# A gated MLP block with local attention on one core: 7-for-8 in the first projection, reloads and stores on another DMA queue, and the last two matrix products exchanged

## The chip, the cores and the metric

The kernel runs on 1 core of a Trainium2 chip. The metric is device time in microseconds (us), lower is better. Each kernel is run several times, beside the kernel before on the same chip.

Engine names follow the profile. PE is TensorE (matmul), PEld its weight loads, DVE VectorE, ACT ScalarE, POOL GpSimd, SP SyncE. A `q` after a name (SPq, ACTq) is that engine's instruction queue issuing a DMA.

## The reference, cut to what matters

```python
# x: [1, 2048, 1024]   wqkv: [1024, 3072]   wo: [1024, 1024]   w1, w3: [1024, 3584]   w2: [3584, 1024]   all bf16
def reference(x, wqkv, wo, w1, w3, w2):
    xn = _layernorm(x)
    q, k, v = split_heads(xn @ wqkv)                 # 32 heads of 32
    # each position sees 8 keys: itself, 2 back, 4 back, ... 14 back
    attn = softmax(mask(einsum("bhsd,bhswd->bhsw", q, k[idx]) * Dh ** -0.5))
    s = einsum("bhsw,bhswd->bhsd", attn, v[idx]) @ wo
    h = silu(xn @ w1) * (xn @ w3)
    g = silu(h @ w2)
    return x + s * g
```

## The kernel before

All large products use a 7-for-8 scheme: a 2x2 block product needs seven block products, if the sums of blocks (`s1`..`s4`, `t1`..`t4`) have been formed on VectorE. The exception is q of the first two chunks of 512 tokens (`q_plain`). The work runs in this order. "Half" is 1024 tokens.

```python
    for st in range(NST):                                  # head: normalise and transpose chunk 0
        ln_tp(0, st, [(xT[:, 0:2], slice(0, 2))], ...)
    q_plain(0, wq0, wq1, ...); q_plain(1, wq0, wq1, ...)   # first q: eight products of eight
    qkv_seven(1, 0, ...) ... qkv_seven(0, 1, ...)          # k, v and the second q
    mlp_up(0, {1: att_step, 6: att_step})                  # "up", half 0; attention runs beside it on DVE
    mlp_down(0)
    att_step()
    wo(0)
    mlp_up(1, {0: att_step, 7: att_step})
    mlp_down(1)
    wo(1)                                                  # the last product
```

First, q, k and v of later chunks are parked in DRAM and reloaded, 1 MB each, on the SP queue. That queue also carries all weight loads. In the trace SP waits 6.6 us there for the copy on POOL that the vT load needs, and issues the loads of q and of weights only after it, at 277.85 and 278.62 us. The code of the reloads:

```python
    def fetch_k(c):
        ...
        nc.gpsimd.tensor_copy(out=kT[:, :, 0:HALO], in_=kT[:, :, CH:CH + HALO])
        nc.sync.dma_start(out=kT[:, :, HALO:], in_=k_dram[c])
        qt[c] = att_tile((NJ, CH), BF16, f"qt{c}")
        nc.sync.dma_start(out=qt[c][:], in_=q_dram[c])

    def fetch_v(c):
        nc.gpsimd.tensor_copy(out=vT[:, :, 0:HALO], in_=vT[:, :, CH:CH + HALO])
        nc.sync.dma_start(out=vT[:, :, HALO:], in_=v_dram[c])
```

Second, in up of half 0 the weights are loaded, summed on VectorE, used, and the sums stored for half 1:

```python
        nc.sync.dma_start(out=wt[:, 0], in_=w1_r[:, :, fc])       # 512 KB; w3 alike
        ...
            nc.vector.tensor_add(st[:, 0], wt[:, 1, 0:KH], wt[:, 1, KH:KT])   # ... four sums
        nc.gpsimd.dma_start(out=s_dram[fb], in_=st[:])            # 1 MB
```

Third, the end of each output tile of `wo`. The store is issued by ScalarE, and the residual x is loaded into a tile that it shares with the product:

```python
        def finish(u, dh, gp, ps, add=None):
            ...
            xo = (k4 if b == 0 else a4)(f"xo{b}{u}{dh}{gp}", (2, 2, CH), BF16)
            nc.sync.dma_start(out=xo[:, 0], in_=rows_(x_flat))
            with hp():
                ...                                               # xo[:, 1] = the product
                nc.vector.tensor_mul(g, xo[:, 1], g)
                nc.vector.tensor_add(g, g, xo[:, 0])
                nc.scalar.dma_start(out=rows_(out_flat), in_=g)
```

## Time and profile before

The median is 767.7 us (3 runs, 765.62 to 767.78). The profiled execution spans 765.8 us. The first lines of its page: busy time of PE, then the span in 40 slices of 19.1 us, in tenths (PE busy, granted PE clock, DMA engines busy).

```profile
...
PE 727.2 (95%) x3381; PEld 352.9 (46%) x3436; DVE 603.0 (79%) x573; ACT 328.5 (43%) x346; POOL 72.7 (9%) x104
...
PE   7999999989999998999999999799999999999994
...
PEclk8999999999999999999999999899999999999998
DMA  9342454574686799969748868445367546453413
...
```

PE is busy 95% of the span. Its row dips in one inner slice, the 26th (479 to 498 us), where the clock row dips too, and in the last. So the time can fall only where PE stands still, runs at half clock, or does work that can be left out. I cut the span into stages at the first matmul of each. Here are three stages of before. The columns are: window, its length, then busy time and instruction count of PE, PEld, DVE, ACT and POOL, then the granted clock, DMA share and GB/s.

```profile
...
core 0: us, PE busy (x) PEld busy (x) DVE busy (x) ACT busy (x) POOL busy (x), PEclk, DMA share, GB/s
173.82:356.06 182.24, 171.98 (x780) 76.25 (x793) 175.06 (x180) 89.70 (x88) 26.34 (x37) 1.00 0.77 257
467.97:645.27 177.30, 170.20 (x770) 76.50 (x784) 152.51 (x117) 90.42 (x89) 9.46 (x17) 0.98 0.55 172
755.78:765.81 10.03, 0.17 (x1) 0.00 (x0) 4.76 (x8) 1.93 (x2) 0.00 (x0) 0.76 0.63 210
...
```

Up of half 0 lasts 182.24 us, with VectorE busy 175.06. Up of half 1 does the same products in 177.30 us. The tail, in which PE has nothing left to do, is 10.03 us. In this trace matmuls with 512 columns start 0.2157 us apart at a granted clock of 1.00, which is called full clock here, and 0.427 us apart at 0.50, half clock (13.3 to 16.9 us). A *stop* in this document is what the spacing of two weight loads exceeds 0.2157 us by.

Where PE waits in the stretch of up of half 0 around 268 to 307 us, and where VectorE does. The columns of the waits view: who waited for whom, us in total, times, longest.

```profile
...
PE em L136 <- DVE st L493: 3.0, 1, 3.0
PE am L136 <- DMA w<-in_B_w_dram: 0.9, 1, 0.9
```

```profile
...
DVE st L493 <- DMA w<-in_B_w_dram: 3.6, 1, 3.6
...
```

The 3.0 us wait for weight sums (`st`) is VectorE's 3.6 us wait for a weight load, passed on. The queues show what that load stood behind. This is the timeline of SP's queue and of POOL in this stretch: start, length, instruction.

```profile
...
277.28 0.53 SPq L365 DMA_DIRECT2D vT<-v_dram  x1
277.85 0.66 SPq L361 DMA_DIRECT2D qt<-q_dram  x1
278.62 0.37 SPq L480 DMA_DIRECT2D w<-in_B_w_dram  x1
...
```

```profile
...
270.75 6.50 POOL L364 COPY vT<-vT 128x128 bf16<-128x128 bf16 x1 [1.51 <-DVE C L412]
...
```

The reload of vT waits for a 6.50 us copy on POOL. The weight load at 278.62 comes behind it and behind the reload of q.

At the border from wo to up of half 1, first ACT, then PE:

```profile
...
479.67 1.48 ACTq L716 DMA_DIRECT2D out_dram<-h_sb  x3
485.50 1.00 ACT L146 COPY bm<-am 128x1024 f32<-128x1024 f32 x1 [8.44 <-DMA out_dram<-h_sb]
...
```

```profile
...
470.44 8.40 DMA xo<-in_A_x_dram
...
479.63 1.15 DVE pt L374
...
484.19 1.23 DVE um L525
...
485.50 1.00 ACT bm L146
...
```

```profile
...
486.55 2.29 PE L136 MATMUL am<-xT,w 128*128 128x512 bf16 x5 [4.55 <-ACT bm L146]
489.06 1.06 PE L136 MATMUL am<-xT,w 128*128 128x512 bf16 x2 [0.22 <-issue]
...
```

ACT stands idle for 8.44 us before the copy that PE needs. In its queue ahead of the copy are three output stores, which wait for VectorE. They are issued from 479.67 to 481.14 us. The bracket names the one of several semaphores that the profile puts last; the chain shows what released the copy at 485.50: VectorE's addition `um`, which ends at 485.42. VectorE itself had waited 3.1 us for a load of residual x (issued at 470.44, 8.40 us to land), and then ran the scores of attention chunk 3 (`pt`, `Es`) ahead of `um`. PE waits 4.55 us and then runs at half clock (granted clock 0.50 from about 484.6 to 491.4 us): its next eight matmuls (eight weight loads; one matmul record is missing) fill 486.55 to 489.92 us, where 8 x 0.2157 us is 1.7. The end of the kernel:

```profile
...
752.33 3.62 PE L136 MATMUL wb<-wt,oT 128*128 128x512 f16 x16
...
756.17 0.97 SPq L708 DMA_DIRECT2D xo<-in_A_x_dram  x2
...
760.28 0.69 DVE L715 TENSOR_TENSOR h_sb<-h_sb,xo 128x1024 bf16<-128x1024 bf16 x1 [0.38 <-DMA xo<-in_A_x_dram]
```

The last two loads of residual x are issued only at 756.17, after PE has finished, because their tiles were in use until then (SP waits 13.7 us there for VectorE's addition, L715). The last addition waits 0.38 us for one.

### The profile page before, as it was taken

The numbers are of one execution on the slowest core, as the hardware profiler recorded it, in microseconds if no ns is written. First come the engines' busy times: TensorE is split into PE (matmuls) and PEld (weight loads), VectorE is DVE, ScalarE is ACT, GpSimd is POOL, SyncE is SP. The second block draws the span as 40 slices with busy tenths as digits, with TensorE's granted clock in tenths as the row PEclk, the third lists the DMA queues.
The fourth block names the chain that finished last, engine by engine and source line by source line (L and its number), as shares of the span: only waits on it lengthen the run. The fifth ranks groups of instructions, "written<-read, shape, count | busy, mean of one in ns | idle before, by whom it ended". The sixth has DMA issues, their size and how long they took to land.

```text
span 765.8 us, 8592 instructions
## 1 busy us (share of the span) xinstructions
PE 727.2 (95%) x3381; PEld 352.9 (46%) x3436; DVE 603.0 (79%) x573; ACT 328.5 (43%) x346; POOL 72.7 (9%) x104
## 2 busy tenths in 40 slices
PE   7999999989999998999999999799999999999994
PEld 3666655554444343444444444344444444444442
DVE  7825997699999998999999568899993699711426
ACT  4786433534444455544121254354565453121232
POOL 0000000130000042300061004000004000000000
PEclk8999999999999999999999999899999999999998
DMA  9342454574686799969748868445367546453413
GB/s 338 115 171 119 179 178 151 158 226 141 228 274 224 217 315 316 286 240 334 258 151 278 312 194 244 138 152 149 140 193 209 175 150 207 145 188 118 140 55 111
DMA packets 115928, 151.56 MB, mean 198 GB/s; under 512 B 4912, under 2 KB 94512, under 8 KB 110000
## 3 DMA queue, kind: packets, MB, share of 16 engines
q1 hardware_dynamic: 101280, 111.16, 45.0%
q0 software_dynamic: 5072, 26.22, 9.7%
q10 hardware_dynamic: 9536, 13.63, 5.0%
q8 instruction: 27, 0.44, 0.3%
q14 instruction: 13, 0.11, 0.0%
HBM read 107.48 MB, written 39.32 MB: 192 GB/s over the span
## 4 chain that ended last, share of the span: by engine, by line
PE 51%; DVE 26%; issue 10%; DMA 9%; ACT 2%; POOL 1%; SPq 0%; ACTq 0%; DVEq 0%; POOLq 0%
PE db L136 9%; PE bm L136 7%; PE de L136 6%; PE da L136 5%; DVE pt L373 4%; PE am L136 4%; PE em L136 4%; DMA w<-in_B_w_dram 4%; PE qp L136 4%; PE bq L136 3%; DVE pt L374 3%; PE aq L136 2%; PE eq L136 2%; DVE um L525 2%; DVE h_sb L535 2%
## 5 line engine op out<-in xcount | busy, mean ns | idle before, releaser
L136 PEld LDWEIGHTS <-h_sb 128*128 128x128 f16 (+1 forms) x944 | 98.9, 105 | 108.6 <-issue 4.9
L136 PEld LDWEIGHTS <-st 128*128 128x128 f16 x896 | 86.9, 98 | 112.0 <-DVE st L493 8.4
L136 PE MATMUL am<-xT,w 128*128 128x512 bf16 x425 | 106.3, 383 | 8.4 <-ACT bm L146 5.3
L136 PEld LDWEIGHTS <-w 128*128 128x128 bf16 x672 | 66.0, 99 | 94.0 <-issue 15.4
L136 PE MATMUL bm<-xs,st 128*128 128x512 f16 x448 | 105.8, 379 | 0.2
L373 DVE TENSOR_TENSOR pt<-qt,kT 128x4096 bf16<-128x4096 bf16 x32 | 73.2, 2287 | 0.5
L136 PE MATMUL db<-wt,h_sb 128*128 128x512 f16 x336 | 73.2, 379 | 0.0
L136 PEld LDWEIGHTS <-wq 128*128 128x128 bf16 (+1 forms) x352 | 50.4, 144 | 31.7 <-issue 7.3
L527 ACT ACTIVATE g<-um 128x1024 bf16<-128x1024 f32 x28 | 29.6, 1057 | 74.3 <-DVE um L525 74.2
L136 PE MATMUL bm<-xs,w 128*128 128x512 f16 x224 | 55.4, 383 | 3.5 <-DVE h_sb L535 3.4
L136 PE MATMUL em<-xs,st 128*128 128x512 f16 x224 | 53.2, 379 | 3.9 <-DVE st L493 3.9
L136 PE MATMUL em<-xT,st 128*128 128x512 bf16 x218 | 52.4, 379 | 0.3
L543 DVE TENSOR_TENSOR h_sb<-h_sb,g 128x2048 bf16<-128x2048 bf16 x28 | 34.1, 1218 | 20.2 <-ACT g L542 20.2
L136 PE MATMUL da<-wt,h_sb 128*128 128x512 bf16 x219 | 48.9, 379 | 0.6 <-DMA wt<-in_B_w_dram 0.3
L405 POOL DMA_DIRECT2D Ep<-pb x64 | 36.9, 584 | 84.8 <-DVE pb L401 81.5
L146 ACT COPY pm<-em 128x1024 f32<-128x1024 f32 x28 | 28.4, 1013 | 28.8 <-PE em L136 28.8
L374 DVE TENSOR_TENSOR pt<-pt 128x2048 bf16<-128x2048 bf16 x32 | 39.0, 1218 | 0.3
L521 ACT ACTIVATE h_sb<-am 128x1024 bf16<-128x1024 f32 x28 | 28.6, 1023 | 20.0 <-PE am L136 20.0
L525 DVE TENSOR_TENSOR um<-em,um 128x1024 f32<-128x1024 f32 x28 | 34.1, 1216 | 3.8 <-PE em L136 2.5
L146 ACT COPY bm<-am 128x1024 f32<-128x1024 f32 x28 | 28.0, 1000 | 20.9 <-DMA out_dram<-h_sb 8.4
L146 ACT COPY um<-bm 128x1024 f32<-128x1024 f32 x28 | 28.4, 1013 | 19.2 <-PE bm L136 19.2
L412 DVE TENSOR_TENSOR B<-Ep,vT 128x4096 bf16<-128x4096 bf16 x16 | 36.5, 2282 | 0.0
(161 smaller groups left out, 978.4 us busy)
## 6 DMA issues: line engine op xcount, KB each, us to landing
w<-in_B_w_dram SPq DMA_DIRECT2D x42, 512.0 KB, 5.3
s_dram<-st POOLq DMA_DIRECT2D x14, 1024.0 KB, 5.1
wt<-t_dram SPq DMA_DIRECT2D x16, 896.0 KB, 6.5
st<-s_dram SPq DMA_DIRECT2D x14, 1024.0 KB, 5.0
wt<-in_B_w_dram SPq DMA_DIRECT2D x12, 896.0 KB, 6.4
w2q<-in_B_w_dram SPq DMA_DIRECT2D x14, 512.0 KB, 4.6
t_dram<-w2q POOLq DMA_DIRECT2D x7, 1024.0 KB, 5.2
wq<-in_A_wqkv_dram SPq DMA_DIRECT2D x6, 1024.0 KB, 7.7
```

What stands on the lines that cost most here:

```text
L136: nc.tensor.matmul(ps, lhsT=lhs[k], rhs=rhs[k], start=(first and k == 0), stop=(k == n - 1), skip_group_check=not first,)
L146: nc.scalar.copy(out=out_, in_=in_)
L373: nc.vector.tensor_mul(p_t[:], q[:], kT[:, :, o:o + CH])
L374: nc.vector.tensor_add(p_t[:, 0:4, :], p_t[:, 0:4, :], p_t[:, 4:8, :])
L405: nc.gpsimd.dma_start(out=pr[c][r:P:NR, :, sq * P:(sq + 1) * P], in_=pb[sq * 32:(sq + 1) * 32, :, :])
L412: nc.vector.tensor_mul(dst, E[:, w, :].unsqueeze(1).to_broadcast([P, NJ, CH]), vT[:, :, o:o + CH])
L521: nc.scalar.activation(out=h_sb[:, f2, 0:CH], in_=pa[:], func=ACTF.Silu)
L525: m = nc.vector.tensor_add(su2[:], pe[:], su2[:])
L527: nc.scalar.activation(out=hl["g"][:, :, CH:], in_=su2[:], func=ACTF.Silu)
L535: m = nc.vector.tensor_add(h_sb[:, f2, CH:], pb[:], sp5[:])
L543: nc.vector.tensor_mul(h_sb[:, f2, :], h_sb[:, f2, :], hl["g"][:])
```

## The change

Its intent: use the 7-for-8 scheme for the first q as well, which takes 16 matmuls out; put the last `wo` ahead of the last down, so that the kernel ends on a cheaper finish; get the reloads out of the weight loads' queue and the early stores out of ScalarE's queue (both go to POOL's queue, which the profile lists as software_dynamic: 26.22 MB in before); and keep PE's clock up with dummy matmuls before the first q. The diff, cut to its core (the renamings and the splitting of `wo` into `wo_prepare` and `wo` are left out):

```diff
+    def spin(ps, n):                        # dummies
+        for k in range(n):
+            nc.tensor.matmul(ps[:, k % 2], lhsT=warm[:, 0:P], rhs=warm[:], start=True, stop=True)
...
     def ln_tp(c, st, dst, busy=0):
         tp = bank2(f"tp{c}_{st}")
+        spin(tp, busy)                      # 5, 0, 1, 1 for the four tiles of chunk 0
...
-        nc.sync.dma_start(out=kT[:, :, HALO:], in_=k_dram[c])
+        nc.gpsimd.dma_start(out=kT[:, :, HALO:], in_=k_dram[c])
...
-        nc.sync.dma_start(out=qt[c][:], in_=q_dram[c])
+        nc.gpsimd.dma_start(out=qt[c][:], in_=q_dram[c])
...
-        nc.sync.dma_start(out=vT[:, :, HALO:], in_=v_dram[c])
+        nc.gpsimd.dma_start(out=vT[:, :, HALO:], in_=v_dram[c])
...  # att_steps: the attention of chunks 2 and 3
         with priority(BG + 20000):
             softmax(2)
+        yield
+        with priority(BG + 30000), behind("wo"):     # not before wo's VectorE work
             scores(3)
-        yield
-        with priority(BG + 30000):
-            values(2)
-            fetch_v(3)
+            values(2, (0, 2, 4))
...  # finish of wo, half 0: x is loaded ahead into its own tile
+        d = h_sb[:, 16 + 2 * n:18 + 2 * n, CH:]
         with hp():
+            to_bf16(d, ps, add)
+            anchor["wo"] = nc.vector.tensor_mul(g, d, g)
+            nc.vector.tensor_add(g, g, xw[u, dh][:, gp])
-            nc.scalar.dma_start(out=rows_(out_flat), in_=g)
+            nc.gpsimd.dma_start(out=out_rows(out_flat, 0, u, dh, gp), in_=g)
...  # finish of the last down; the wo product waits in so, the residual in xr
+    def gated(u, dh, gp, i_=slice(0, 2)):
+        g = g_tile(1, u, dh, gp)[:, i_]
+        with hp():
+            nc.vector.tensor_mul(g, so[u][:, dh, gp, i_], g)
+            nc.vector.tensor_add(g, g, xr[u][:, dh, gp, i_])
+            nc.sync.dma_start(out=out_rows(out_flat, 1, u, dh, gp)[:, i_], in_=g)
...  # head
-    q_plain(0, wq0, wq1, xk(xT[:, 0], xT[:, 1]), mid1)
-    q_plain(1, wq0, wq1, xk(b12[:], xT[:, 2]))
+    for t, (w0, w1_, ws) in enumerate(((wq0, wq1, sq), (wk0, wk1, sk))):
+        first_two(...)                      # a11*b11 + a12*b21 for q and k: needs chunk 0 alone
+    qkv_seven(0, 0, wq0, wq1, sq, None, snap[0:2])
...
-    nc.sync.dma_start(out=x_dram[:, 0:2], in_=xT1[:, 0:2])      # three stores, to gpsimd
+    nc.gpsimd.dma_start(out=x_dram[:, 0:2], in_=xT1[:, 0:2])
...
-    mlp_up(1, {0: att_step, 7: att_step})
-    mlp_down(1)
-    wo(1)
+    mlp_up(1, {0: att_step, 6: att_step})
+    wo_prepare(1)
+    wo(1, finish1)
+    residual()
+    mlp_down(1, gated)
```

More of the change, by code (lines that the diff above doesn't have):

```diff
@@ L126 @@
     nc.vector.memset(warm[:], 0.0)
+    def spin(ps, n):
+        for k in range(n):
+            nc.tensor.matmul(ps[:, k % 2], lhsT=warm[:, 0:P], rhs=warm[:], start=True, stop=True)
     for i in range(4):
-        wps = bank2(f"warm{i}")
-        for h in range(2):
-            for _ in range(2 if i < 2 else 1):
-                nc.tensor.matmul(wps[:, h], lhsT=warm[:, 0:P], rhs=warm[:], start=True, stop=True)
+        spin(bank2(f"warm{i}"), 4 if i < 2 else 2)
     def mm(ps, lhs, rhs, first):
@@ L152, in flush, with first_two, seven @@
             pend.pop(0)()
-    def seven(key, A, B, e11, e12, e22, e21):
+    def first_two(key, A, b11, b21, snap, e11, mid=lambda: None, busy=0):
+        pa = []
+        for g in range(2):
+            pa.append(bank2(f"a{key}{g}"))
+            spin(pa[g], busy if g == 0 else 0)
+            for i in I:
+                mm(pa[g][:, i], A[g][0][i], b11, True)
+            act_copy(snap[g], pa[g][:])
+        mid()
+        for g in range(2):
+            for i in I:
+                mm(pa[g][:, i], A[g][1][i], b21, False)
+            e11[g](pa[g])
+    def seven(key, A, B, e11, e12, e22, e21, snap=None):
         a11, a12, a22, s1, s2, s3, s4 = A
         b11, b21, b22, t1, t2, t3, t4 = B
-        pa = bank2(f"a{key}")
-        for i in I:
-            mm(pa[:, i], a11[i], b11, True)
+        if snap is None:
+            pa = bank2(f"a{key}")
+            for i in I:
+                mm(pa[:, i], a11[i], b11, True)
         pe = bank2(f"e{key}")
@@ L163, in seven @@
         pb = bank2(f"b{key}")
-        act_copy(pb[:], pa[:])
+        act_copy(pb[:], pa[:] if snap is None else snap)
         sp5 = k4(f"p{key}")
         act_copy(sp5[:], pe[:])
-        for i in I:
-            mm(pa[:, i], a12[i], b21, False)
-        e11(pa)
+        if snap is None:
+            for i in I:
+                mm(pa[:, i], a12[i], b21, False)
+            e11(pa)
         flush()
@@ L239, in ln_act, with ln_tp @@
             nc.scalar.activation(out=x_t, in_=x_t, func=ACTF.Identity, bias=v[:, 3, i:i + 1], scale=v[:, 2, i:i + 1])
-    def ln_tp(c, st, dst, copy=None):
+    def ln_tp(c, st, dst, busy=0):
         tp = bank2(f"tp{c}_{st}")
+        spin(tp, busy)
         for kt in range(KT):
@@ L249, in ln_tp @@
         for d, s_ in dst:
-            (copy or nc.scalar.copy)(out=d[..., cols], in_=tp[:, s_].rearrange("p a (k t) -> p a k t", k=KH))
+            nc.scalar.copy(out=d[..., cols], in_=tp[:, s_].rearrange("p a (k t) -> p a k t", k=KH))
+        return tp
     def xn_sums(b11, b21, b12, b22, o):
@@ L299, in qkv_dst, with qkv_copy, f, qkv_seven @@
         return park(t, c, j0, f"pk{t}_{c}_{j0}")
-    def qkv_seven(t, b, w0, w1_, st, mid=None):
-        for g in range(2):
-            outs = {}
-            def cp(key, c, j0):
-                def f(ps, *a):
-                    d, fin = qkv_dst(t, c, j0)
-                    with hp():
-                        if a:
-                            nc.vector.tensor_add(d, ps[:], a[0][:])
-                        else:
-                            nc.scalar.copy(out=d, in_=ps[:])
-                        fin()
-                return f
-            c0, c1 = 2 * b, 2 * b + 1
+    def qkv_copy(t, c, j0):
+        def f(ps, *a):
+            d, fin = qkv_dst(t, c, j0)
+            with hp():
+                if a:
+                    nc.vector.tensor_add(d, ps[:], a[0][:])
+                else:
+                    nc.scalar.copy(out=d, in_=ps[:])
+                fin()
+        return f
+    def qkv_seven(t, b, w0, w1_, st, mid=None, snaps=None):
+        c0, c1 = 2 * b, 2 * b + 1
+        for g in range(2):
+            cp = lambda c, j0: qkv_copy(t, c, j0)
             seven(f"q{t}{b}{g}", qkv_A(w0, w1_, st, g), (B0, B1)[b],
-                  cp("11", c0, 2 * g), cp("12", c1, 2 * g), cp("22", c1, 4 + 2 * g), cp("21", c0, 4 + 2 * g))
+                  cp(c0, 2 * g), cp(c1, 2 * g), cp(c1, 4 + 2 * g), cp(c0, 4 + 2 * g),
+                  None if snaps is None else snaps[g])
             if mid is not None:
@@ L325, in qkv_load @@
         return wt
-    def q_plain(c, w0, w1_, xk, mid=None):
-        wv = [w.rearrange("p k (c j) -> p k j c", j=NJ) for w in (w0, w1_)]
-        for j0 in range(0, NJ, 2):
-            ps = bank2(f"qp{c}_{j0}")
-            for i in I:
-                mm(ps[:, i], [wv[kt // 4][:, kt % 4, j0 + i, :] for kt in range(KT)], xk, True)
-            d, fin = qkv_dst(0, c, j0)
-            with hp():
-                nc.scalar.copy(out=d, in_=ps[:])
-                fin()
-            if mid is not None:
-                mid(j0 // 2)
     qt = {}
@@ L405, in softmax, with values @@
                 nc.gpsimd.dma_start(out=pr[c][r:P:NR, :, sq * P:(sq + 1) * P], in_=pb[sq * 32:(sq + 1) * 32, :, :])
-    def values(c):
+    def values(c, pairs=(0, 2, 4, 6)):
         E = pr[c]
@@ L414, in values @@
         A = oT[:, c % 2]
-        pvmul(A, 0)
-        B = att_tile((NJ, CH), BF16, f"B{c}_1")
-        pvmul(B[:], 1)
-        nc.vector.tensor_add(A, A, B[:])
-        for w0 in (2, 4, 6):
-            B = att_tile((NJ, CH), BF16, f"B{c}_{w0}")
-            C = att_tile((NJ, CH), BF16, f"C{c}_{w0}")
-            pvmul(B[:], w0)
-            pvmul(C[:], w0 + 1)
-            nc.vector.tensor_add(B[:], B[:], C[:])
+        for w0 in pairs:
+            B = att_tile((NJ, CH), BF16, f"B{c}_{w0}")
+            if w0 == 0:
+                pvmul(A, 0)
+                pvmul(B[:], 1)
+            else:
+                C = att_tile((NJ, CH), BF16, f"C{c}_{w0}")
+                pvmul(B[:], w0)
+                pvmul(C[:], w0 + 1)
+                nc.vector.tensor_add(B[:], B[:], C[:])
             nc.vector.tensor_add(A, A, B[:])
@@ L461, in att_steps @@
             softmax(3)
+            values(2, (6,))
+            fetch_v(3)
             values(3)
@@ L574, in g_tile, with mlp_down @@
         return h_sb[:, f0:f0 + 2, col:col + CH]
-    def mlp_down(b):
+    def mlp_down(b, done=lambda *a: None, mid=lambda n: None):
         NQ = 7
@@ L639, in mlp_down @@
         product(pb, lst(s2), rhs, False, snap2)
+        mid(0)
         for gp in G2:
@@ L642, in mlp_down @@
                 silu(g_tile(b, 0, 0, gp), pa[gp][:])
+            done(0, 0, gp)
         rhs = rhs_tiles("t", t=T3)
@@ L653, in c22 @@
                 silu(g_tile(b, 1, 1, gp), sp5[:])
+            done(1, 1, gp)
         product(pe, lst(s1), rhs, True, c22)
@@ L661, in c12, with wo_prepare @@
                 silu(g_tile(b, 0, 1, gp), su2[gp][:])
+            done(0, 1, gp)
         product(pe, lst(s4), rhs, False, c12)
         rhs = rhs_tiles("t", t=T4)
+        mid(1)
         def c21(gp):
-            with hp():
-                silu(g_tile(b, 1, 0, gp), pb[gp][:])
+            for i in [slice(0, 2)] if b == 0 else [slice(0, 1), slice(1, 2)]:
+                with hp():
+                    silu(g_tile(b, 1, 0, gp)[:, i], pb[gp][:, i])
+                done(1, 0, gp, i)
         product(pb, lst(a22), rhs, False, c21)
-    def wo(b):
+    wx = {}
+    def wo_prepare(b):
         wot = []
@@ L678, in wo, with sums @@
             nc.sync.dma_start(out=wot[h][:], in_=wo_r[:, h * 4:(h + 1) * 4, :])
-        t4 = r8.tile([P, 4, CH], FP16, tag="r8", name=f"wt{b}")[:]
-        t1, t2, t3 = [h16[:, 14 + 4 * i:18 + 4 * i, 0:CH] for i in range(3)]
         b11, b12, b21, b22 = wot[0][:, :, 0:CH], wot[0][:, :, CH:D], wot[1][:, :, 0:CH], wot[1][:, :, CH:D]
-        with hp():
+        if b == 0:
+            t1, t2, t3 = [h16[:, 14 + 4 * i:18 + 4 * i, 0:CH] for i in range(3)]
+            t4 = r8.tile([P, 4, CH], FP16, tag="r8", name=f"wt{b}")[:]
+            free = rows(0, 6)
+        else:
+            t1, t2, t3, t4 = [xs[:, i] for i in range(4)]
+            free = xT[:].rearrange("p a k n -> p (a k n)")
+        s1 = free[:, 0:4 * CH].bitcast(FP16).rearrange("p (j n) -> p j n", j=4)
+        su2 = [free[:, (1 + gp) * 4 * CH:(2 + gp) * 4 * CH].bitcast(FP32).rearrange("p (i n) -> p i n", i=2) for gp in G2]
+        a11, a12, a21, a22 = oT[:, 0, 0:4, :], oT[:, 0, 4:8, :], oT[:, 1, 0:4, :], oT[:, 1, 4:8, :]
+        s2, s4, s3 = o16[:, 0, 0:4, :], o16[:, 0, 4:8, :], o16[:, 1, 0:4, :]
+        wx[b] = (a11, a12, a21, a22, s1, s2, s3, s4), (b11, b12, b21, b22, t1, t2, t3, t4), su2
+        if b == 0:
             nc.vector.tensor_sub(t1, b12, b11)
+            nc.vector.tensor_add(s1, a21, a22)
             nc.vector.tensor_sub(t2, b22, t1)
+    def wo(b, finish):
+        (a11, a12, a21, a22, s1, s2, s3, s4), (b11, b12, b21, b22, t1, t2, t3, t4), su2 = wx[b]
+        def sums(gp):
+            if gp > 0:
+                return
+            flush()
+            if b > 0:
+                nc.vector.tensor_sub(t1, b12, b11)
+                nc.vector.tensor_add(s1, a21, a22)
+                nc.vector.tensor_sub(t2, b22, t1)
+            nc.vector.tensor_sub(s3, a11, a21)
             nc.vector.tensor_sub(t3, b22, b12)
             nc.vector.tensor_sub(t4, b21, t2)
-        a11, a12, a21, a22 = oT[:, 0, 0:4, :], oT[:, 0, 4:8, :], oT[:, 1, 0:4, :], oT[:, 1, 4:8, :]
-        s2, s4, s3 = o16[:, 0, 0:4, :], o16[:, 0, 4:8, :], o16[:, 1, 0:4, :]
-        s1 = rows(0, 2, FP16).rearrange("p (j n) -> p j n", j=4)
-        with hp():
-            nc.vector.tensor_add(s1, a21, a22)
-            nc.vector.tensor_sub(s3, a11, a21)
         def product(ps, lhs, rhs, first, after=None):
@@ L700, in product @@
                     after(gp)
-        def finish(u, dh, gp, ps, add=None):
-            g0 = ((2 * b + u) * NST + gp * 2) * P
-            cols = slice(dh * CH, (dh + 1) * CH)
-            xo = (k4 if b == 0 else a4)(f"xo{b}{u}{dh}{gp}", (2, 2, CH), BF16)
-            g = g_tile(b, u, dh, gp)
-            rows_ = lambda ap: ap[g0:g0 + 2 * P, cols].rearrange("(i p) n -> p i n", p=P)
-            nc.sync.dma_start(out=xo[:, 0], in_=rows_(x_flat))
-            with hp():
-                if add is None:
-                    nc.scalar.copy(out=xo[:, 1], in_=ps[:])
-                else:
-                    nc.vector.tensor_add(xo[:, 1], ps[:], add)
-                nc.vector.tensor_mul(g, xo[:, 1], g)
-                nc.vector.tensor_add(g, g, xo[:, 0])
-                nc.scalar.dma_start(out=rows_(out_flat), in_=g)
         pa = [bank2(f"wa{b}_{gp}") for gp in G2]
-        product(pa, a11, b11, True)
+        product(pa, a11, b11, True, sums)
         pb = [bank2(f"wb{b}_{gp}") for gp in G2]
@@ L727, in wo @@
             nc.vector.tensor_sub(s4, a12, s2)
-        su2 = []
-        def snap2(gp):
-            su2.append(rows(2 + 2 * gp, 2, FP32).rearrange("p (i n) -> p i n", i=2))
-            act_copy(su2[gp], pb[gp][:])
-        product(pb, s2, t2, False, snap2)
-        product(pb, s3, t3, False)
-        pe = [bank2(f"we{b}_{gp}") for gp in G2]
-        def c22(gp):
-            sp5 = k4(f"wsp{b}_{gp}")
-            act_copy(sp5[:], pe[gp][:])
-            finish(1, 1, gp, pb[gp], sp5[:])
-        product(pe, s1, t1, True, c22)
+        pe = [bank2(f"we{b}_{gp}") for gp in G2]
@@ L744, in wo, with out_rows @@
+        sp5 = [k4(f"wsp{b}_{gp}") for gp in G2]
+        product(pe, s1, t1, True, lambda gp: act_copy(sp5[gp][:], pe[gp][:]))
+        product(pb, s2, t2, False, lambda gp: act_copy(su2[gp], pb[gp][:]))
+        product(pb, s3, t3, False, lambda gp: finish(1, 1, gp, pb[gp], sp5[gp][:]))
         product(pe, s4, b22, False, lambda gp: finish(0, 1, gp, pe[gp], su2[gp]))
         product(pb, a22, t4, False, lambda gp: finish(1, 0, gp, pb[gp]))
+    def out_rows(ap, b, u, dh, gp):
+        g0 = ((2 * b + u) * NST + gp * 2) * P
+        return ap[g0:g0 + 2 * P, dh * CH:(dh + 1) * CH].rearrange("(i p) n -> p i n", p=P)
@@ new lines, in to_bf16, with finish0 @@
+    def to_bf16(d, ps, add):
+        if add is None:
+            nc.scalar.copy(out=d, in_=ps[:])
+        else:
+            nc.vector.tensor_add(d, ps[:], add)
+    xw = {}
+    def finish0(u, dh, gp, ps, add=None):
+        if (u, dh) not in xw:
+            x2 = xw[u, dh] = k4(f"xw{u}{dh}", (2, 2, CH), BF16)
+            for i in I:
+                nc.sync.dma_start(out=x2[:, i], in_=out_rows(x_flat, 0, u, dh, i))
+        g = g_tile(0, u, dh, gp)
+        n = {(0, 0): 0, (1, 1): 2, (0, 1): 4, (1, 0): 0}[u, dh] + gp
+        d = h_sb[:, 16 + 2 * n:18 + 2 * n, CH:]
+        with hp():
+            to_bf16(d, ps, add)
+            anchor["wo"] = nc.vector.tensor_mul(g, d, g)
+            nc.vector.tensor_add(g, g, xw[u, dh][:, gp])
+            nc.gpsimd.dma_start(out=out_rows(out_flat, 0, u, dh, gp), in_=g)
@@ new lines, with finish1 @@
+    so = {}
+    def finish1(u, dh, gp, ps, add=None):
+        if u not in so:
+            so[u] = att_tile((2, 2, 2, CH), BF16, f"so{u}")
+        with hp():
+            to_bf16(so[u][:, dh, gp], ps, add)
+    def gated(u, dh, gp, i_=slice(0, 2)):
+        g = g_tile(1, u, dh, gp)[:, i_]
+        with hp():
+            nc.vector.tensor_mul(g, so[u][:, dh, gp, i_], g)
+            nc.vector.tensor_add(g, g, xr[u][:, dh, gp, i_])
+            nc.sync.dma_start(out=out_rows(out_flat, 1, u, dh, gp)[:, i_], in_=g)
@@ L749, with residual @@
+    xr = {}
+    def residual():
+        for u in range(2):
+            xr[u] = att_tile((2, 2, 2, CH), BF16, f"xr{u}")
+            for dh in range(2):
+                for gp in range(2):
+                    nc.sync.dma_start(out=xr[u][:, dh, gp], in_=out_rows(x_flat, 1, u, dh, gp))
     x_load(0)
     wq0 = qkv_load(0, 0)
+    x_load(1)
     wq1 = qkv_load(0, 1)
-    x_load(1)
     for st in range(NST):
@@ L755 @@
     qt[0] = att_tile((NJ, CH), BF16, "qt0")
-    for st in range(NST):
-        ln_tp(0, st, [(xT[:, 0:2], slice(0, 2))], nc.vector.tensor_copy if st == NST - 1 else None)
+    tps = [ln_tp(0, st, [], busy=(5, 0, 1, 1)[st]) for st in range(NST)]
+    for a in I:
+        for st in range(NST):
+            (nc.vector.tensor_copy if st < 2 else nc.scalar.copy)(
+                out=xT[:, a, :, st * P:(st + 1) * P], in_=tps[st][:, a].rearrange("p (k t) -> p k t", k=KH),
+            )
     wk0 = qkv_load(1, 0)
@@ L761 @@
     sk = [sk[:, q] for q in range(3)]
-    xk = lambda a, b_: [a[:, k, :] for k in range(KH)] + [b_[:, k, :] for k in range(KH)]
     b12 = k4("b12", (KH, CH), BF16)
@@ L765, with tp1 @@
     ln_dve(1, [2, 3])
-    def mid1(g):
-        for st in {1: [0, 1], 2: [2, 3]}.get(g, []):
-            ln_tp(1, st, [(b12[:].unsqueeze(1), slice(0, 1)), (xT[:, 2:3], slice(1, 2))])
-    q_plain(0, wq0, wq1, xk(xT[:, 0], xT[:, 1]), mid1)
+    sq = rows(20, 6, FP16).rearrange("p (q k n) -> p q k n", q=3, k=4)
+    sq = [sq[:, q] for q in range(3)]
+    snap = [rows(12 + 2 * i, 2, FP32).rearrange("p (i n) -> p i n", i=2) for i in range(4)]
+    def tp1(*sts):
+        for st in sts:
+            ln_tp(1, st, [(b12[:].unsqueeze(1), slice(0, 1)), (xT[:, 2:3], slice(1, 2))])
+    for t, (w0, w1_, ws) in enumerate(((wq0, wq1, sq), (wk0, wk1, sk))):
+        first_two(f"f{t}", [qkv_A(w0, w1_, ws, g) for g in range(2)], B0[0], B0[1],
+                  snap[2 * t:2 * t + 2], [qkv_copy(t, 0, 2 * g) for g in range(2)],
+                  *((lambda: None, 4) if t == 0 else (lambda: tp1(2, 3), 0)))
+        if t == 0:
+            tp1(0, 1)
+    qkv_sums(wq0, wq1, sq)
+    xn_sums(xT[:, 0], xT[:, 1], b12[:], xT[:, 2], xs)
     qkv_sums(wk0, wk1, sk)
-    xn_sums(xT[:, 0], xT[:, 1], b12[:], xT[:, 2], xs)
-    q_plain(1, wq0, wq1, xk(b12[:], xT[:, 2]))
+    qkv_seven(0, 0, wq0, wq1, sq, None, snap[0:2])
     for c in (2, 3):
@@ L777 @@
         for sts in ([0, 1], [2, 3]):
-            (ln_dve if c == 2 else ln_act)(c, sts)
+            ln_dve(c, sts)
     def mid(g):
@@ L786, in mid @@
                 ln_tp(c, st, [(xT1[:, 2:4], slice(0, 2))])
-    qkv_seven(1, 0, wk0, wk1, sk, mid)
+    qkv_seven(1, 0, wk0, wk1, sk, mid, snap[2:4])
     wv0 = qkv_load(2, 0)
@@ L791 @@
     xn_sums(xT1[:, 0], xT1[:, 1], xT1[:, 2], xT1[:, 3], xs1)
-    nc.sync.dma_start(out=x_dram[:, 0:2], in_=xT1[:, 0:2])
-    nc.sync.dma_start(out=x_dram[:, 2], in_=xT1[:, 3])
-    nc.sync.dma_start(out=xs_dram[:], in_=xs1)
+    nc.gpsimd.dma_start(out=x_dram[:, 0:2], in_=xT1[:, 0:2])
+    nc.gpsimd.dma_start(out=x_dram[:, 2], in_=xT1[:, 3])
+    nc.gpsimd.dma_start(out=xs_dram[:], in_=xs1)
     sva = r8.tile([P, 2, 4, CH], FP16, tag="r8", name="sva")
@@ L808 @@
     mlp_up(0, {1: att_step, 6: att_step})
-    mlp_down(0)
+    mlp_down(0, mid=lambda n: att_step() if n == 0 else wo_prepare(0))
     nc.sync.dma_start(out=xT[:], in_=x_dram[:])
     nc.sync.dma_start(out=xs[:], in_=xs_dram[:])
-    att_step()
-    wo(0)
-    mlp_up(1, {0: att_step, 7: att_step})
-    mlp_down(1)
-    wo(1)
+    wo(0, finish0)
+    mlp_up(1, {0: att_step, 6: att_step})
[3 more added lines that the diff above has]
+    mlp_down(1, gated)
 _INS = ['A_x', 'A_wqkv', 'A_wo', 'B_x', 'B_w1', 'B_w3', 'B_w2']
```

## The prediction

> **What bounds it now.** TensorE. The page has PE busy 727 of 765.8 us. In the PE timeline warm 512-column matmuls start every 0.2157 us. Gaps between weight-load starts beyond that sum to about 34 us, mostly here:
> - Head: first q matmul at 13.3 us, released by a DVE copy of xT. Until 16.9 us matmuls start every 0.427 us (half clock): 1.9 us lost on the first q.
> - MLP up, half 0 (168-368 us): about 14 us, waits for DVE or a weight load. The largest, 3.3 us at 291 us, goes back in the chain to a 6.5 us POOL copy of vT, behind which the SP queue held weight loads. DVE is 99% busy here except in 250-300 us (43.3 of 50).
> - wo half 0 to up half 1: PE stops 4.7 us at 481.6 us. In the ACT timeline the copy it waits for stands behind three output stores issued from ACT, which wait for DVE. Eleven half-clock matmuls follow: 7 us together.
> - Tail: last matmul ends near 755.9 us, span 765.8: 9.9 us.
>
> **What changes, in us.**
> 1. First q as 7-for-8: 16 matmuls less, -3.45. Half-width xT copies (0.6 instead of 1.2 us): first q near 12.4, -0.9. Dummies fill idle PE slots and should hold the full clock: -1.9. [...] New: q's operand sums (4x1.2 us DVE) precede x's sums; I put t1 at about 29.4 us, t2 near 32, PE arriving at 28: +2.3. Net -4.
> 2. k/v/q reloads on POOL: weight loads no longer queue behind them. -4.5, capped by the DVE idle time there (6.7). Bytes stay the same.
> 3. Stores of wo half 0 on POOL, none in ACT's way; scores(3) held behind wo's DVE work: -6.8.
> 4. Attention finishes inside up half 1: about 111 us DVE plus 14x3.6 us of MLP work in 169 us, and wo's first two products give 14 more. It fits. But DVE's order puts wo's t2 sum, needing a late wo load, ahead of two evacuations of the last up block: +2; denser DVE elsewhere: +1.
> 5. Tail: after the last down matmul a 512-wide SiLU (0.6), multiply and add (0.4 each), one store (2.5 plus 1 to the end): 5.7 instead of 9.9: -4.2.
> Score sums of chunk 2 move into down half 0; their scores ended 3 us before that point: 0.
>
> Sum -16.5, so about 751; I say 752 us, as new stalls are likelier than gains. Range 746 to 759. Faster by over 2%: 0.50; within: 0.48; slower: 0.02.
>
> **Right if the profile shows:** first q near 12.4 us at 0.216 us spacing; a PE wait for DVE of 1-4 us near 28-32; no 3 us wait for weight sums in up half 0; no 4.7 us PE stop or half clock entering up half 1; PE gap under 4 us from up half 1 to wo to down; last matmul to end below 6.5 us.
>
> **Wrong if:** POOL, in order, holds s_dram/t_dram stores behind reloads, so tiles free later and weight loads slip; saturated DVE takes up the gain in up half 0; attention of chunk 3 is late and PE waits over 5 us before wo half 1; the clock still drops between dummies.

The sum: -4 - 4.5 - 6.8 + 2 + 1 - 4.2 = -16.5. The -1.9 has its size from the trace of before: the clock is at 0.50 from the first q matmul at 13.27 us to 16.97, and half of that is 1.85 us. That the dummies would hold the full clock was the author's estimate; e5 and e11 test it. The half-width xT copies took 0.60 us on ScalarE and 0.68 on VectorE in after (estimated 0.6). The lengths in term 5 are estimates too, for which it names no source. The nearest figures in the trace of before are 1.02 us for an activation and 0.68 for a multiplication of 128x1024, twice the width, and a median of 2.5 us for stores of 256 KB (k); the "plus 1" has none. In after they came to 0.59 us (SiLU), 0.42 (each of multiply and add) and 1.7 (the store, 128 KB, from issue to landing), and from there to the end of the span about 1.

## The result

The changed kernel is correct and takes 755.15 us (median of 4 runs, 754.35 to 757.4). Before takes 767.74 us in the same rounds. The ratio is 0.9846, with a 95% interval of 0.9818 to 0.9874. It is faster by 1.5%, so within the 2% band. The experiments ran in three further calls, each on its own chip. Across calls I therefore compare ratios, or times at the same granted clock.

The stages, in us, from the first matmul of each stage in the two traces. "Last two" is wo and down of half 1, in either order. The predicted column is from the prediction's terms; its -6.8, +2 and +1 all fall on the last four stages.

| stage | before | after | change | predicted |
|---|---|---|---|---|
| head, to the first q matmul | 13.27 | 12.43 | -0.84 | -4 with qkv |
| qkv | 160.55 | 156.73 | -3.82 | |
| up, half 0 | 182.24 | 182.22 | **-0.02** | **-4.5** |
| down, half 0 | 87.46 | 87.09 | -0.37 | 0 |
| wo, half 0 | 24.45 | 24.17 | -0.28 | 0 |
| up, half 1 | 177.30 | 172.89 | -4.42 | -6.8 + 1 |
| last two | 110.51 | 111.53 | +1.03 | +2 |
| tail | 10.03 | 5.39 | -4.64 | -4.2 |
| span | 765.81 | 752.45 | -13.36 | -16.5 |

The lines of after that answer to those of before. The page:

```profile
...
PE 725.4 (96%) x3431; PEld 348.2 (46%) x3431; DVE 620.2 (82%) x602; ACT 320.5 (43%) x335; POOL 88.6 (12%) x124
...
PE   8999999989999998999999999999999999999997
...
PEclk9999999999999999999999999999999999999999
DMA  9352544655776798879855996444367545634531
...
```

The inner dip of PE and of the clock is gone, and the last slice has 7 tenths instead of 4. The DMA row still reads 7 to 9 from the 14th to the 20th slice. The windows of the same three stages:

```profile
...
core 0: us, PE busy (x) PEld busy (x) DVE busy (x) ACT busy (x) POOL busy (x), PEclk, DMA share, GB/s
169.16:351.38 182.22, 172.69 (x794) 76.13 (x792) 175.22 (x180) 89.71 (x88) 28.67 (x40) 1.00 0.78 257
462.64:635.53 172.89, 169.47 (x785) 75.76 (x784) 160.13 (x120) 88.03 (x87) 15.96 (x23) 1.00 0.52 168
747.06:752.45 5.39, 0.16 (x1) 0.00 (x0) 1.61 (x4) 1.08 (x2) 0.00 (x0) 0.75 0.14 49
...
```

Up of half 0 is as long as before to 0.02 us, with the same GB/s and VectorE as busy. The waits in the same stretch (now 264 to 303 us, since the stage starts 4.7 us sooner):

```profile
...
PE am L137 <- DMA w<-in_B_w_dram: 3.1, 2, 2.2
PE em L137 <- DVE st L500: 0.6, 1, 0.6
```

```profile
...
DVE st L500 <- DMA w<-in_B_w_dram: 3.2, 1, 3.2
...
```

The 3.0 us wait for sums has shrunk to 0.6, as predicted. In its place PE waits 3.1 us for weight loads themselves: before 3.0 + 0.9 = 3.9 us, after 3.1 + 0.6 = 3.7. The queues:

```profile
...
272.16 0.37 SPq L487 DMA_DIRECT2D w<-in_B_w_dram  x1
...
```

```profile
...
266.21 6.50 POOL L370 COPY vT<-vT 128x128 bf16<-128x128 bf16 x1 [1.51 <-DVE C L418]
272.65 0.53 POOL L367 DMA_DIRECT2D qt<-q_dram  x1
273.17 0.91 POOL L371 DMA_DIRECT2D vT<-v_dram  x1
...
```

The weight load no longer stands behind the POOL copy. From the start of the stage it is issued at 272.16 - 169.16 = 103.0 us, against 278.62 - 173.82 = 104.8 before: only 1.8 us sooner. It could not go sooner: its tile came free only at 272.14, with PE's last read of it. The two 1 MB reloads are issued within 1.0 us of it, on the other queue, and are in flight together with it: q took 7.0 us from issue to landing, vT 9.9, and no weight load from 255 to 305 us less than 4.1. A POOL copy of this shape (128x128) is not always 6.50 us long: the traces have it at 0.29 us (before, 123.11), 0.40 (e8) and 12.84 (before, 383.94). VectorE was busy throughout the long ones of before (6.50 of 6.50 us and 12.80 of 12.84). No run tests that this is the cause.

The border to up of half 1:

```profile
...
474.93 1.00 ACT L147 COPY bm<-am 128x1024 f32<-128x1024 f32 x1 [0.19 <-PE am L137]
...
```

```profile
...
474.73 1.89 PE L137 MATMUL em<-xs,st 128*128 128x512 f16 x8
476.45 1.89 PE L137 MATMUL am<-xT,w 128*128 128x512 bf16 x8
...
```

The copy that had an idle ACT for 8.44 us before it now waits for nothing but PE's own product (0.19 us). PE goes on without a stop: eight matmuls take 1.72 us from start to start. The tail:

```profile
...
742.75 4.48 PE L137 MATMUL db<-wt,h_sb 128*128 128x512 f16 x20
...
747.26 1.08 ACT L625 ACTIVATE h_sb<-db 128x512 bf16<-128x512 f32 x2 [4.96 <-PE db L137]
...
749.14 0.42 DVE L793 TENSOR_TENSOR h_sb<-h_sb,xr 128x512 bf16<-128x512 bf16 x1
```

The end is now two half-size SiLUs on ScalarE and short VectorE work, and nothing waits for a load.

### The profile page after: what moved, and what is told of

The parts are those of the page before. It is cut to its first block, busy times and chain, and to the rows that moved or that the text cites. A ratio compares the mean times of both kernels' runs of the same rounds, so it can differ in the third digit from the quotient of the medians. Undisturbed runs are those within 1.5% of the kernel's fastest.

```text
span 752.4 us, 8657 instructions
## 1 busy us (share of the span) xinstructions
PE 725.4 (96%) x3431; PEld 348.2 (46%) x3431; DVE 620.2 (82%) x602; ACT 320.5 (43%) x335; POOL 88.6 (12%) x124
## 3 DMA queue, kind: packets, MB, share of 16 engines
q0 software_dynamic: 8208, 41.43, 15.1%
## 4 chain that ended last, share of the span: by engine, by line
PE 45%; DVE 32%; issue 13%; DMA 6%; ACT 2%; POOL 1%; SPq 0%; DVEq 0%; ACTq 0%; POOLq 0%
PE db L137 10%; PE de L137 6%; PE da L137 6%; DVE pt L379 5%; PE bq L137 5%; PE bm L137 4%; DMA w<-in_B_w_dram 3%; DVE pt L380 2%; PE eq L137 2%; DVE um L532 2%; DVE h_sb L542 2%; PE am L137 2%; PE wb L137 2%; PE em L137 2%; PE aq L137 2%
## 5 line engine op out<-in xcount | busy, mean ns | idle before, releaser
L137 PEld LDWEIGHTS <-h_sb 128*128 128x128 f16 (+1 forms) x976 | 102.2, 105 | 112.2 <-issue 4.8
L137 PEld LDWEIGHTS <-w 128*128 128x128 bf16 x672 | 65.2, 97 | 93.9 <-issue 11.9
L137 PEld LDWEIGHTS <-wq 128*128 128x128 bf16 (+1 forms) x288 | 41.3, 144 | 24.8 <-issue 4.2
L431 DVE TENSOR_TENSOR oT<-oT,B 128x4096 bf16<-128x4096 bf16 x16 | 36.6, 2287 | 0.1
```

What stands on the lines that cost most here:

```text
L137: nc.tensor.matmul(ps, lhsT=lhs[k], rhs=rhs[k], start=(first and k == 0), stop=(k == n - 1), skip_group_check=not first,)
L431: nc.vector.tensor_add(A, A, B[:])
```

## The experiments

Twelve kernels ran. All passed the check of correctness. That includes e9, which loads an eighth of a tile and computes a wrong result on purpose: the check did not catch it. Times are medians.

| run | what it is | us | ratio to before (95%) |
|---|---|---|---|
| changed kernel | | 755.15 | 0.9846 (0.9818 to 0.9874) |
| e1 | after, reloads back on SP | 756.07 | 0.9850 (0.9818 to 0.9883) |
| e2 | before, reloads on POOL | 766.7 | 0.9979 (0.9947 to 1.0010) |
| e3 | after, w2 loads on POOL | 756.14 | 0.9839 (0.9808 to 0.9869) |
| e4 | before, stores of wo half 0 on POOL | 762.44 | 0.9934 (0.9904 to 0.9964) |
| e5 | after, no dummies | 759.44 | 0.9900 (0.9868 to 0.9931) |
| e6 | after, stores of wo half 0 on ACT | **752.89** | **0.9821 (0.9795 to 0.9847)** |
| e7 | after, wo behind down again | 756.73 | 0.9868 (0.9843 to 0.9894) |
| e8 | after, v reload later | 756.15 | 0.9856 (0.9825 to 0.9888) |
| e9 | e8, q reload of 128 KB (wrong result) | 751.91 | 0.9816 (0.9793 to 0.9839) |
| e10 | e8, q reload sooner | 759.67 | 0.9916 (0.9896 to 0.9937) |
| e11 | before, dummies alone | 766.24 | 0.9997 (0.9972 to 1.0022) |
| e12 | e10 with e6 | 756.89 | 0.9874 (0.9853 to 0.9895) |

### Which queue issues the reloads: e1 and e2

My theory at this point was still the prediction's: the reloads hold up the weight loads on SP. The rival: the DMA engines are full in this stretch (mean share 0.91 in before, 268 to 307 us, and 0.95 in after, 264 to 303), and the issuing queue makes no difference.

```diff
# e1, from after (six places: reloads of k, q, v and three stores of x, xs); e2 is the opposite edit in before
-        nc.gpsimd.dma_start(out=qt[c][:], in_=q_dram[c])
+        nc.sync.dma_start(out=qt[c][:], in_=q_dram[c])
```

> The changed kernel with only the k/v/q reloads and the x/xs stores put back on the SP queue (DVE and PE order unchanged). Theory A (in the MLP-up stage of half 0 the reloads on POOL bought nothing, because a weight load is held there by something else): within 1 us of the changed kernel, 754 to 757 us. Rival B (the prediction's step: reloads hold weight loads, worth 4.5 us, and something else in the change gave it back): 758.5 to 761 us, with a 3 us PE wait for weight sums near 286 us.

> The kernel before with only the reloads and the x/xs stores moved to the POOL queue. Theory A: within 1 us of the kernel before, the 3.0 us PE wait near 291 us turning into a wait for a weight load a few us later. Rival B: 4 to 5 us faster, near 763 us.

The ratio with the reloads back on SP is 0.9850, without the edit 0.9846. In before, the edit gives 0.9979, so 1.6 us less with an interval that reaches zero. In e2's profile up of half 0 is 181.57 us, 0.67 less than before's. In e1's it is 184.38, 2.2 more than after's. But in that profile PE ran at half clock from 291.76 to 295.17 us, which costs half of 3.41 us, so 1.7 of the 2.2. By profiles and medians the move to POOL is worth one or two microseconds at most. The intervals exclude the predicted 4.5, but not 2 to 4. A PE wait for sums did come back in e1 (3.4 us), as the rival expectation had it, without its cost in time.

### Another thing on the queue: e3

A variant of the theory: the weight loads now stand behind the w2 loads on SP, which wait for a store to land.

```diff
-                nc.sync.dma_start(out=tiles["t"][:, i], in_=w2_q[:, fb + i])
+                nc.gpsimd.dma_start(out=tiles["t"][:, i], in_=w2_q[:, fb + i])
```

> The changed kernel with the seven pairs of w2 loads of MLP-up half 0 moved from SP to POOL; DVE and PE orders are the same. Theory A (a weight load stands in the SP queue behind a w2 load, which waits for the previous t_dram store to free its tile): the 4.0 us of PE waits for weight loads in that stage go, and the 4.7 us that DVE waits for them; 3 to 4.5 us faster than the changed kernel, near 751.5. Rival C (the 16 DMA engines are full there, the bytes decide): unchanged within 1 us, the same 2 us wait for a weight load near 298 us. Rival D (DVE, busy 175 of 182 us in that stage, decides): the waits for loads go, waits for DVE grow instead, under 1.5 us faster.

The ratio is 0.9839: no change. Up of half 0 is 183.76 us in the profile, with a half-clock window from 291.14 to 294.56 us. PE's waits in the stretch:

```profile
...
PE em L137 <- DVE st L500: 2.9, 1, 2.9
PE am L137 <- DMA w<-in_B_w_dram: 0.8, 1, 0.8
```

They sum to 2.9 + 0.8 = 3.7 us, exactly after's sum, with the load in the way gone. One 512 KB weight load, issued at 273.6, landed 16.3 us later; the DMA row reads 9 tenths in every slice from 275.7 us until it landed. Before has the same: the load issued at 279.03 took 15.0 us, at a mean DMA share of 0.96. The median of these loads over the whole of before is 5.3 us. This variant fell too. What stayed was the rival: bytes in flight, not places in a queue.

### Bytes in flight: e8, e9 and e10

e8 moves the vT copy on POOL and its 1 MB reload from 266 us to 321 (the copy takes 0.40 us there). The lines that set the anchor `("s", 11)` are left out of this cut.

```diff
             values(0)
-            fetch_v(1)
         yield
...
+        yield
+        with priority(BG + 15000):
+            with behind(("s", 11)):
+                fetch_v(1)
```

> The changed kernel with the second vT copy and its 1 MB reload moved on the POOL queue from about 266 us to about 315 us, where its reader comes at 344 us; no other instruction changes place. Theory C' (the reload burst shares the 16 DMA engines with the weight loads of up blocks 9 and 10 wherever it is issued, so its queue does not matter but its time does): the waits of 2.6 and 1.0 us at 297 to 303 us go, 2 to 3.5 us faster than the changed kernel, near 752.5. Rival (the t_dram and s_dram stores set the loads' time): unchanged within 1 us, the same waits there.

e9 is e8 with one DMA made smaller; all instructions keep their order. e10 keeps the size and issues that DMA 85 us sooner (181.24 us in its trace, 266.45 in e8's), into a tile that is free by then.

```diff
# e9
-        nc.gpsimd.dma_start(out=qt[c][:], in_=q_dram[c])
+        n = 1 if c == 2 else NJ
+        nc.gpsimd.dma_start(out=qt[c][:, 0:n], in_=q_dram[c, :, 0:n])
# e10
-        qt[c] = att_tile((NJ, CH), BF16, f"qt{c}")
+        qt[c] = oT[:, 1] if c == 2 else att_tile((NJ, CH), BF16, f"qt{c}")
```

> Wrong result on purpose: as e8_after_v_late, but the 1 MB reload of chunk 2's q is cut to 128 KB (the scores that use it get it broadcast), so 0.9 MB fewer bytes move around 266 to 275 us and nothing else changes place. Theory (the reloads' bytes share the 16 DMA engines with up0's weight loads, whichever queue issues them, so moving their issue to POOL bought nothing): the 3.9 us wait for weights at 271.6 us falls to about 1.3 or less, up0 from 181.6 to about 178.7, and the time lies about 3 us below e8's. Rival (up0 is held by VectorE, busy 175 of its 182 us, and by the base traffic of weights): up0 stays at 181 to 182 and the time at e8's.

> Correct: as e8_after_v_late, and the reload of chunk 2's q goes to another tile and is issued about 65 us sooner, before up0's dense stretch of weight loads. Theory (bytes in the wrong stretch): up0 about 179, the time about 3 us below the changed kernel's 755.2, near 752. Rival (VectorE or base traffic holds up0): up0 181 to 182.5 and the time 754 to 756.

PE's and VectorE's waits for weight loads in the stretch from 264 to 303 us, e8 first:

```profile
...
PE am L137 <- DMA w<-in_B_w_dram: 3.6, 1, 3.6
...
DVE st L503 <- DMA w<-in_B_w_dram: 2.7, 1, 2.7
...
```

```profile
...
PE am L137 <- DMA w<-in_B_w_dram: 2.2, 1, 2.2
...
DVE st L505 <- DMA w<-in_B_w_dram: 1.2, 1, 1.2
...
```

```profile
...
PE am L137 <- DMA w<-in_B_w_dram: 0.9, 1, 0.9
...
```

In e8 two waits at 297 to 303 us went, and the one at 271.6 us, 0.9 us in after, grew to 3.6. There the q reload, no longer held behind the POOL copy, is issued 1.65 us after a weight load, which then took 10.9 us to land instead of 8.3. So e8 gained 0.65 us in the stage and nothing in time; 2 to 3.5 us had been expected.

The row to read is PE's sum in this stretch, and VectorE's wait for loads:

| run | reloads in the stretch | VectorE waits for loads | PE waits, all |
|---|---|---|---|
| before | q and v, on SP | 3.6 | 3.9 |
| after | q and v, on POOL | 3.2 | 3.7 |
| e8 | q, on POOL | 2.7 | 3.6 |
| e9 | an eighth of q, on POOL | 1.2 | 2.2 |
| e10 | none | 0 | 0.9 |

e9 differs from e8 in the size of one transfer alone, and PE waits 1.4 us less. The stage goes from 181.57 to 180.17 us: the right direction and half of the 2.9 us that I expected. In time, the ratio is 0.9816 against 0.9856. At the same mean granted clock of 1.000, e9 took 751.64 us and e8 took 753.59, 753.62 and 754.56: two to three microseconds. (Most of e8's median is its other three runs; see the clock below.) The two ratios' intervals overlap slightly, and the spans of the two profiles differ by 1.3 us. VectorE's work is the same in both (175.21 and 175.24 us busy), so a less disturbed VectorE is not the reason. So the bytes of the q reload are shown as the cause of 1.4 of e8's 3.6 us. What still holds PE for 2.2 us in e9 I did not take apart.

e10 confirms this in the stretch and loses overall. With no reload left there, PE waits 0.9 us. But the later v reload, now issued at 335.7 instead of 321.8 (its POOL copy took 8.06 us here), meets the last stores of up. VectorE's order had changed too, so this is not a clean single edit. SP's queue and PE at the border to down:

```profile
...
SPq L597 <- DMA t_dram<-w2q: 11.9, 1, 11.9
...
```

```profile
...
PE da L137 <- DMA wt<-in_B_w_dram: 6.3, 1, 6.3
...
```

SP waits 11.9 us for a store of w2 sums to land (11.1 us; in e8 it took 4.2) before it may issue the first weights of down. PE stands 6.3 us, and runs at half clock afterwards (mean granted clock 0.80 from 345 to 362 us, at a DMA share of 0.95). The run takes 759.67 us, 0.9916. My expectation of 752 was wrong: bytes moved out of one full stretch met others elsewhere, where the queue did have a dependency to hold.

### Stores and ScalarE: e4, e6 and e12

```diff
# e4, from before
-                nc.scalar.dma_start(out=rows_(out_flat), in_=g)
+                (nc.gpsimd if b == 0 else nc.scalar).dma_start(out=rows_(out_flat), in_=g)
# e6, from after
-            nc.gpsimd.dma_start(out=out_rows(out_flat, 0, u, dh, gp), in_=g)
+            nc.scalar.dma_start(out=out_rows(out_flat, 0, u, dh, gp), in_=g)
```

> The kernel before with only the eight output stores of wo half 0 moved from the ACT queue to POOL. Theory (the ACT queue, held by stores that wait for DVE, stopped PE 4.7 us and led to 2.3 us of half clock): 6 to 7 us faster than before, near 761, no half clock between 481 and 491 us. Rival (scores of chunk 3 ahead of the output sums on DVE hold the evacuations themselves): less than 3 us faster, a PE wait of 2 us or more stays near 482 us.

> The changed kernel with only the stores of wo half 0 put back on the ACT queue. If the queue alone decides, as moving it alone in the kernel before (4.9 us of up half 1) suggests: 4 to 7 us slower than the changed kernel, 759 to 762, a PE stop of over 3 us entering up half 1. Rival (scores of chunk 3 held behind wo's sums let the sums end early, so the stores wait for nothing): under 2 us slower, no half clock.

In before, moving the stores alone gives a ratio of 0.9934, so 5.1 us; 6 to 7 had been expected. Up of half 1 falls from 177.30 to 172.47 us. The 4.71 us stop is gone, and no half clock follows; the longest stop near the border is 1.20 us, at 472.9, another place. The late copy, in e4:

```profile
...
481.73 1.00 ACT L146 COPY bm<-am 128x1024 f32<-128x1024 f32 x1 [0.76 <-PE am L136]
...
```

So moving the stores removes this stop. By which path is less clear, for the prediction's was that the stores stand in ACT's queue, and in before they had been issued 4.4 us ahead of the copy. Two other things changed in e4. The last two loads of residual x landed in 4.6 and 5.0 us instead of 8.6 and 8.4, and VectorE did not wait for them. And VectorE's order changed: `um` stands ahead of the last two score operations (2.7 us in before), and ends at 479.88. So e4 does not test the rival in its expectation either. Which of the two counts, and whether fewer stores in flight made the loads faster, no run separates.

e6 puts the stores back on ScalarE in the changed kernel, and the stop does not return; 4 to 7 us more had been expected. Up of half 1 is 171.42 us, against 172.89 in after, and the ratio is 0.9821 against 0.9846. There, scores(3) is held behind wo's VectorE work, and x is loaded ahead into its own tile. With these two in place the stores need not move. No run has the hold alone, so whether it would do by itself is not shown. e6 is the fastest correct kernel here, 752.89 us, although its interval overlaps that of after. The same edit on e10 points the same way:

> Correct, a candidate for the best: e10_q_early_v_late with finish0's two stores issued from ScalarE, as in e6_after_store_act. If both gains add: about 749.5 to 750.5. If up0 gains nothing from the earlier q reload: as e6, 752 to 753.

e12 takes 756.89 us, 0.9874 against e10's 0.9916. Why ACT does better than POOL is open: the edit also changes VectorE's order and where ScalarE's exponentials stand among its other work, and I did not separate these. As a best candidate e12 missed, for it carries e10's stop (5.38 us here).

### The order of the last two products: e7

```diff
# e7, from after, cut: finish0 also gets b, and stores half 1 on SP
-    wo_prepare(1)
-    wo(1, finish1)
-    residual()
-    mlp_down(1, gated)
+    mlp_down(1, mid=lambda n: wo_prepare(1) if n == 1 else None)
+    wo(1, partial(finish0, b=1))
```

> The changed kernel with wo of half 1 put back behind the last down product, gated and stored as half 0 is, stores on SP. Theory (what the reordering buys is the tail): 5.39 us from last matmul to end becomes 9 to 10, the wait of 1.0 us before wo goes: 3 to 4 us slower than the changed kernel, near 758.5. Rival (the earlier tail is won by the split SiLU and SP stores, the order itself costs PE stalls): under 1.5 us slower.

The tail is 7.27 us: 1.88 more than after, but 2.76 less than before. The last two products take 110.51 us, 1.03 less than in after, as before. So the order nets 1.88 - 1.03 = 0.85 us in the profile, and 1.6 us in the medians, with intervals that overlap; 3 to 4 us had been expected. The larger part of the tail's gain came with the order in which `wo` takes its products, the residual loaded ahead, and the stores on SP. I did not separate these three.

### The dummies: e5 and e11

```diff
# e5, from after: the dummies of tp and of the first q left out
# e11, from before: the same eleven dummies put in
+        if c == 0:
+            spin(tp, (5, 0, 1, 1)[st])
...
+            if c == 0 and j0 == 0:
+                spin(ps, 4)
```

> The changed kernel without the eleven dummy matmuls between the transposes and ahead of the first q (the twelve warm-up ones stay). Theory (they hold the full clock): the clock falls to half before the first q, as in the kernel before, the first q matmuls come every 0.427 us until about 17 us, the first q starts within 0.4 us of 12.4 us: 1.5 to 2.2 us slower than the changed kernel, near 757. Rival (the idle gaps are too short to drop the clock, or the half clock is hidden by the wait for the sums at 28 us): within 0.7 us of the changed kernel.

> The kernel before plus the 11 dummy matmuls alone; the order of VectorE is the same. Theory (the dummies take the half clock out of the first q): the stretch of half clock at about 10 to 17 us is gone and the time falls by about 1.9 us, to some 765.9. Rival (the start waits for VectorE's normalisation and the loads anyway): no change within 0.5 us, 767.3 to 768.

Without dummies the changed kernel takes 759.44 us, a ratio of 0.9900 against 0.9846. Its head and qkv are 3.1 us longer in the profile (172.28 against 169.16). But not through half clock in the first q: in e5's profile the low clock lay ahead of it, in 10 to 13.5 us (mean granted clock 0.61 from 10 to 14.36 us, and 1.00 from there to 20), and PE waited 2.9 us for the normalised x. The fourth tile of x also landed later in that profile (7.46 us instead of 6.04), and the transposes of it start 1.5 us later, which is about half of the 3.1. So that the size was roughly as foreseen is luck, the path was not foreseen, and small reorderings on PE and VectorE are mixed in.

In before, the half clock in the place that the theory names is gone with the dummies. Head and qkv fell from 173.82 to 171.70 us, 2.1 us. These are windows of e11, the first after the first q, the second around 291 us:

```profile
...
11.60:20.00 8.40, 7.61 (x39) 4.85 (x37) 7.74 (x18) 3.40 (x5) 0.00 (x0) 1.00 1.05 390
286.00:300.00 14.00, 10.99 (x43) 4.41 (x42) 10.40 (x12) 6.38 (x7) 2.16 (x4) 0.88 0.93 314
...
```

The clock is 1.00 where before had 10.15 to 16.97 us at half. But PE ran part of 286 to 300 us at half clock in this run (mean 0.88), and the stage grew by 1.4 us. Over the runs the ratio is 0.9997 (0.9972 to 1.0022): no gain is shown, and 2 us are just not excluded.

### What the clock does to run-to-run comparison

In e8 the granted clock explains most of the spread. Its six timed runs fall in two groups. Three at a mean clock of 1.000 took 753.59 to 754.56 us. Three at 0.991 took 757.75 to 758.0. That is 0.009 x 754 = 6.8 us of clock lost, if it were all used; the groups differ by about 4 us. In the profiles, the stretches at half clock are once or twice 3.41 us long (3.41 in e1 and 3.42 in e3 near 291 us, 6.8 in before from 484.6 to 491.4, and 6.82 from 10.15 to 16.97); 3.41 us is called a window here. Each (the head and the end apart) follows a PE stop, but not each stop is followed by one. All stops of 1.5 us or more after the first q, in all fourteen profiles:

| length of the stop, us | stops | followed by half clock |
|---|---|---|
| 1.5 to 2.6 | 29 | 3, for one window |
| 3.2 to 3.9 | 7 | 4, for one window |
| 4.4 to 6.7 | 5 | 5, for two windows |

In the middle row the very same stop, near 290 us, went both ways: 3.33 us in before and 3.35 in e4 without, 3.27 in e11 and 3.31 in e3 with. What decides it no run shows. A stop of 3.2 to 3.9 us was, in these profiles, a lottery ticket (4 of 7) for half of 3.41 = 1.7 us on top.

## Why the prediction was right, and where it was not

The prediction said 752 us, 746 to 759, and "within 2%" at 0.48 against "faster" at 0.50. The measured 755.15 lies inside the range, 3 us above the centre, and inside the 2% band; the slightly likelier "faster" did not come. The sizes by term are from one profile each; the first matmul of up of half 0 comes at 173.8 to 175.1 us in before, e2 and e4, which share a head, and at 169.0 to 171.1 in the changed kernel and its variants that keep the dummies. By the profile's stages, the terms:

1. **Head and first q, -4: measured -4.65. Right in size.** The first q matmul is at 12.43 us (predicted near 12.4), and PE's wait for sums at 28 to 31 us was 1.2 us (predicted 2.3). What the dummies were to do is shown in the start of before (e11: clock 1.00 from 11.60 to 20.00 us, -2.1 us in head and qkv), not in the total.

2. **"k/v/q reloads on POOL: weight loads no longer queue behind them. -4.5": measured -0.02. This step failed.** The reading of the trace was right: the load did stand behind a POOL copy. The inference was wrong. Freed, the weight load was issued only 1.8 us sooner, and met the reloads in the DMA engines (mean share 0.91 in the stretch before, 0.95 after). The prediction wrote "Bytes stay the same" beside this term and drew nothing from it. The traces have 257 GB/s in the stage both before and after, at a DMA share of 0.77 and 0.78, and e1, e2 and e3 show no effect of the queue clear of noise. That the bytes decide, e9 shows for a part, by taking some away: 1.4 us of PE's wait. The check that I had named for this step, no 3 us wait for sums, came true while the step failed, because the wait had only moved to another product. A check should have been on PE's sum of waits.

3. **"Stores of wo half 0 on POOL, none in ACT's way; scores(3) held: -6.8": the stop went as predicted, the path was only half right, the size was off.** Up of half 1 lost 4.42 us; with the +1 of term 4 the prediction had -5.8. The stop and its half clock are gone, but they were counted at full value, while new small stops came in the same stage: 1.72 us at 525 us and about 0.7 us at 553 and at 601. The stores in ACT's way were not what PE waited for last: the copy was released by VectorE, which was late from a load of x and from scores(3). The two parts were named in one breath as if both were needed; e6 shows that, with scores(3) held and x loaded ahead, moving the stores is not.

4. **"+2" before the last products: measured +1.03**, a single stop at 637 us. Attention finished in time.

5. **Tail, -4.2: measured -4.64. Right in size.** The prediction costed the new ending and did not say what the order alone is worth. e7 shows that the order nets 0.85 us in the profile, and the rest comes from the other parts of the ending.

Predicted -16.5, measured -13.36 in the span. The difference is 3.1 us: term 2 promised 4.5 too much, the other terms together 1.3 too little. That the total came within 3.1 us is so in part luck.

## What to carry to other kernels

Before moving a DMA to another queue, ask whether the wait behind it is for its turn to be issued or for its bytes. Here the DMA engines were at 0.91 and 0.95 of the stretch. Three changes of queue (e1, e2, e3) showed no effect clear of noise, and 0.9 MB fewer in it (e9) took PE's waits there from e8's 3.6 us to 2.2. What helped here was fewer bytes, not another queue. The whole reload moved out of the stretch (e10, not a clean single edit) took the waits to 0.9, but PE then stood 6.3 us at the border to down: so the new place has to be checked as carefully as the old. Test a step by the sum of PE's waits in its stage, not by the disappearance of one wait, since a wait for one operand can become a wait for another, as here. Where the profile names one of several semaphores, look up when that one was really done. When a change bundles two cures for one stop, undo each alone: here one of them was not needed, and the kernel without it was the fastest.
